# Reading a compressive memory with sixteen row-tiled products in place of four full ones, and keeping the memory on GpSimd

## The chip, the cores and the metric

The kernel runs on one core of one Trainium2 chip. The metric is the device time of one execution in microseconds (us); each comparison runs both kernels on the same chip.

## The reference, cut to what matters

A transformer layer: layer norm, attention with a compressive memory over four segments of 512 tokens (32 heads of 32 dimensions), then a gated MLP. Only the memory matters here.

```python
for s in range(4):                       # segments
    ...
    pq  = phi(qs)                        # phi(t) = t + 1 if t > 0 else exp(t)
    num = einsum('bhld,bhde->bhle', pq, M)
    den = einsum('bhld,bhd->bhl',  pq, z)[..., None] + 1e-06
    o   = g * (num / den) + (1 - g) * a_dot      # g: a gate per head
    M   = M + einsum('bhld,bhle->bhde', phi(ks), vs)
    z   = z + einsum('bhld->bhd', phi(ks))
```

## The kernel before

The heads are worked on in groups of four, which fill the 128 partitions: 8 groups a segment, 32 in all. I call them groups 0 to 31; groups 8 to 31 read the memory (24 reads), groups 0 to 23 add to it. A product in a *row tile* uses only 32 of the 128 rows (`tile_position` in the code says which); a *full-height* one uses all 128. The main loop interleaves group n's logits, group n-1's value read and state, and "filler" matmuls (projections of later groups, the output projection `wo`).

```python
def logits(n, rnd):                       # three rounds; each head is a 32-row tile with its own PSUM bank 0..3
    ...
            pe.matmul(PS[:, i, o:o + w], qk[32 * i:32 * (i + 1), 1, ...], qk[32 * i:32 * (i + 1), 0, ...],
                      start=True, stop=True, tile_position=(32 * i, 0))
    if rnd == 2 and n >= NQ:
        mem(n)
    act.activation(e[:, :, 0:wid], PS[:, 0:4, 0:wid], ACTF.Exp, scale=float(SCALE))
    ...  # causal mask on GpSimd (affine_select)
    if rnd == 2 and n >= NQ:
        mem_norm(n)

def mem(n):                               # block-diagonal memory: 128 rows x (4 heads x 33)
    c = n % NQ
    for cq in range(4):
        pe.matmul(PS[:, cq, 256:388], PQK[n % 2][:, 0, cq * 128:(cq + 1) * 128], MZB[:, c, :, 0:33],
                  start=True, stop=True)

def norm(n):                              # normalise the value read (PSUM banks 4 and 5), add the memory part
    ...  # VectorE: rd, rd, ta, otok

def state(n):
    ...
    b = next_bank()                       # banks 6 and 7 in turn, shared with the fillers
    for tcl in range(4):
        pe.matmul(PS[:, b, 0:132], PK[n % 3][:, tcl, :], V[:, tcl, 4 * c:4 * c + 4, 0:33], ...)
    if s == 0:
        dve.tensor_copy(MSUM[:, c, :], PS[:, b, 0:132])
    else:
        dve.tensor_tensor(MSUM[:, c, :], MSUM[:, c, :], PS[:, b, 0:132], ALU.add)
    dve.tensor_tensor(MZB[:, c, :, 0:33], MSUM..., MASKG[:, c, :, :], ALU.mult)

# main loop, group n:
    logits(n, 0); fill(f1); pv(n - 1)     # value read; ends with norm(n - 1)
    logits(n, 1); state(n - 1); fill(f2)
    logits(n, 2); fill(f3); fill(f4)      # f3 takes the bank that state() used
```

Waits are derived from a record of which 32-byte cells of on-chip memory (and which PSUM bank) each operation touched. And a PSUM bank counts as one thing: the filler behind the memory read may not start before VectorE has emptied the bank of the state product.

The softmax here doesn't subtract the row's maximum and nothing guards it: scores larger than these inputs give would overflow.

## Time and profile before

| | before |
|---|---|
| time, median | 801.87 us at first; 801.75 us with the runs beside the changed kernel |
| span in the profile | 800.1 us |
| first logit product to last (the attention stretch) | 283.45 us |
| 24 steps from last logit product over the memory read to the first filler | 11.43 us in all; 457 ns usually |

The head of the page of the kernel before, and its chain of waits:

```profile
span 800.1 us, 12483 instructions
...
PE 794.0 (99%) x5369; PEld 380.5 (48%) x5369; DVE 379.8 (47%) x769; ACT 297.6 (37%) x347; POOL 128.9 (16%) x241
...
PE 96%; DVE 3%; issue 0%; ACT 0%
```

TensorE (PE) sets the time; its queue is 96% of the path. A saving counts only if it shortens the queue of matmuls, and a delay elsewhere counts only if PE meets it.

The timeline of the kernel before at one memory read (start, duration, engine, operation, count):

```profile
152.71 0.29 PE L209 MATMUL ps<-qk 32*128 32x256 bf16 x4
...
152.93 0.41 PE L209 MATMUL ps<-mzb,pqk 128*128 128x132 bf16 x4
...
153.18 3.62 PE L209 MATMUL ps<-wv,xnT 128*128 128x512 bf16 x16
```

From the logits (152.71) to the filler (153.18) is 0.47 us; counted from the last of the four logit products, by single records, it is 457 ns: 210 to the first memory product, then 70, 59, 59 and 59.

The timeline of the kernel before at a read that came late (brackets: how long the engine was idle, and who ended it):

```profile
113.87 0.28 DVE L209 TENSOR_TENSOR msum<-msum,ps 128x132 f32<-128x132 f32 x1
114.19 0.30 DVE L209 TENSOR_TENSOR mzb<-msum,maskg 128x132 bf16<-128x132 f32 x1
114.20 1.36 POOL L209 TENSOR_SCALAR_AFFINE_SELECT e<-e 128x512 bf16<-128x512 bf16 x2 [2.51 <-ACT e L209]
...
114.21 0.29 PE L209 MATMUL ps<-qk 32*128 32x256 bf16 x4
...
114.54 0.23 PEld L209 LDWEIGHTS ps<-mzb,pqk 128*128 128x128 bf16 x4 [0.24 <-DVE mzb L209]
```

Group 11 reads the memory of its own heads, written eight groups earlier, yet it waits for the mask product of group 10, which ends at 114.49. The buffer has 272 bytes a group, not a multiple of 32, so a group and its neighbour share a cell. Four reads of 24 come 104 to 120 ns late this way.

The groups of instructions of the kernel before that the change touches (busy us, mean ns of one | idle us before):

```profile
L209 PE MATMUL ps<-mzb,pqk 128*128 128x132 bf16 x96 | 9.8, 225 | 0.2
...
L209 DVE TENSOR_TENSOR mzb<-msum,maskg 128x132 bf16<-128x132 f32 x24 | 7.5, 312 | 0.8
...
L209 DVE TENSOR_TENSOR msum<-msum,ps 128x132 f32<-128x132 f32 x16 | 4.5, 283 | 0.0
```

And the busy times of the kernel before in the stretch from the first logits of group 11 to those of group 13 (length, then busy us of each engine):

```profile
core 0: us, PE busy (x) PEld busy (x) DVE busy (x) ACT busy (x) POOL busy (x), PEclk, DMA share, GB/s
...
108.66:127.91 19.25, 19.20 (x194) 9.64 (x195) 17.68 (x41) 13.68 (x12) 7.44 (x14) 1.00 0.52 123
```

VectorE (DVE) is busy 17.68 us of 19.25 here, 92%, where its mean over the kernel is 47%.

### The profile page before, as it was taken

To read this page: it belongs to the slowest core of one execution; us is meant where nothing else is said; L and a number is where in the kernel's file an instruction comes from. 1 tells how busy PE (TensorE), PEld (TensorE's weight loads), DVE (VectorE), ACT (ScalarE), POOL (GpSimd) and SP (SyncE) were. 2 spreads that over 40 slices of the span, in tenths; PEclk is the share of its full clock that TensorE was granted. 3 is DMA by queue.
4 is the path that set the end of the run, shared out by engine and by line. 5 is a ranking of instruction groups with operands and counts; after the bars stand their busy time and mean duration, and the time that the engine had idled before them with its cause. 6 is when DMAs were issued, how large, how long until landed. Compare 5 with 4: busy or idle time off the path is not lost.

```text
span 800.1 us, 12483 instructions
## 1 busy us (share of the span) xinstructions
PE 794.0 (99%) x5369; PEld 380.5 (48%) x5369; DVE 379.8 (47%) x769; ACT 297.6 (37%) x347; POOL 128.9 (16%) x241
## 2 busy tenths in 40 slices
PE   8999999999999999999999999999999999999998
PEld 4454545555454445455544444444444444444444
DVE  6775688579844775844562000053234323323432
ACT  5777877787788675133333333100000000000000
POOL 3543333333333331100131000000000000000000
PEclk9999999999999999999999999999999999999999
DMA  9661535363515324511116000650270143021002
GB/s 294 180 161 53 93 81 122 84 106 86 92 31 127 113 54 114 157 47 53 53 53 132 1 0 1 205 105 7 79 132 1 33 116 69 0 66 47 1 7 86
DMA packets 125000, 64.79 MB, mean 81 GB/s; under 512 B 94992, under 2 KB 113936, under 8 KB 124944
## 3 DMA queue, kind: packets, MB, share of 16 engines
q1 hardware_dynamic: 124944, 63.99, 33.1%
q8 instruction: 42, 0.69, 0.4%
q14 instruction: 14, 0.11, 0.0%
HBM read 32.51 MB, written 8.39 MB: 51 GB/s over the span
## 4 chain that ended last, share of the span: by engine, by line
PE 96%; DVE 3%; issue 0%; ACT 0%
PE ps L209 96%; DVE stats L209 1%; DVE ta L209 0%; DVE otok L209 0%; DVE hch L209 0%; ACT e L209 0%; DVE rd L209 0%; DVE pqk L209 0%; DVE lno L209 0%; DVE mzb L209 0%; DVE etmp L209 0%; DVE mv L209 0%; DVE rdm L209 0%; DVE msum L209 0%; DVE xnT L209 0%
## 5 line engine op out<-in xcount | busy, mean ns | idle before, releaser
L209 PE MATMUL ps<-wspT,z 128*128 128x512 bf16 x896 | 194.0, 379 | 0.0
L209 ACT ACTIVATE e<-ps 128x2048 bf16<-128x2048 f32 (+1 forms) x96 | 152.8, 1591 | 49.5 <-PE ps L209 49.0
L209 PEld LDWEIGHTS ps<-wspT,z 128*128 128x128 bf16 x896 | 87.7, 98 | 105.7
L209 DVE TENSOR_TENSOR tmpg<-ps,brow 128x512 f32<-128x512 f32 x56 | 38.7, 691 | 197.1 <-DMA brow<-in_B_b_sp_dram 105.2
L209 POOL TENSOR_SCALAR_AFFINE_SELECT e<-e 128x512 bf16<-128x512 bf16 x128 | 83.5, 664 | 178.9 <-ACT e L209 178.7
L209 PE MATMUL ps<-win,hnT 128*128 128x448 bf16 x512 | 98.3, 352 | 0.0
L209 PE MATMUL ps<-w_out,yT 128*128 128x512 bf16 (+2 forms) x462 | 97.4, 373 | 0.0
L209 PE MATMUL ps<-hnT,win 128*128 128x512 bf16 x448 | 96.9, 379 | 0.0
L209 PEld LDWEIGHTS ps<-win,hnT 128*128 128x128 bf16 x512 | 49.8, 98 | 46.3 <-issue 0.2
L209 PEld LDWEIGHTS ps<-w_out,yT 128*128 128x128 bf16 x462 | 44.7, 98 | 52.4
L209 PEld LDWEIGHTS ps<-hnT,win 128*128 128x128 bf16 x448 | 43.9, 98 | 52.8
L209 PE MATMUL ps<-xnT,wk 128*128 128x512 bf16 x256 | 60.8, 380 | 0.0
L209 PE MATMUL ps<-xnT,wq 128*128 128x512 bf16 x256 | 60.6, 379 | 0.0
L209 PE MATMUL ps<-wv,xnT 128*128 128x512 bf16 x256 | 59.3, 379 | 0.1
L209 ACT ACTIVATE z<-ps 128x448 bf16<-128x448 f32 x60 | 32.5, 543 | 69.5 <-PE ps L209 69.5
L209 PE MATMUL ps<-wo,oT 128*128 128x512 bf16 x256 | 57.9, 379 | 0.0
L209 ACT ACTIVATE z1T<-ps 128x512 bf16<-128x512 f32 x56 | 33.4, 597 | 63.3 <-PE ps L209 63.3
L209 DVE TENSOR_TENSOR fin<-fin,ps 128x512 bf16<-128x512 bf16 (+2 forms) x33 | 22.2, 671 | 71.2 <-DMA fin<-out_dram 39.2
L209 DVE BATCH_NORM_STATS2 zst<-z 128x6 f32<-128x448 bf16 x64 | 38.9, 620 | 30.1 <-ACT z L209 30.1
L209 PEld LDWEIGHTS ps<-v,e 128*128 128x128 bf16 x1280 | 37.3, 96 | 9.1 <-issue 1.7
L209 DVE TENSOR_TENSOR yT<-tmpg,z1T 128x512 bf16<-128x512 f32 x56 | 38.8, 692 | 1.9
L209 PE MATMUL ps<-v,e 128*128 128x33 bf16 x1280 | 38.4, 177 | 0.0
(83 smaller groups left out, 576.1 us busy)
## 6 DMA issues: line engine op xcount, KB each, us to landing
xch<-in_A_x_dram SPq DMA_DIRECT2D x16, 256.0 KB, 3.0
xr<-in_A_x_dram SPq DMA_DIRECT2D x16, 256.0 KB, 3.5
out_dram<-hch SPq DMA_DIRECT2D x16, 256.0 KB, 2.5
fin<-out_dram SPq DMA_DIRECT2D x16, 256.0 KB, 2.7
out_dram<-fin SPq DMA_DIRECT2D x31, 128.0 KB, 1.7
win<-in_B_w_in_dram SPq DMA_DIRECT2D x4, 896.0 KB, 5.2
w_out<-in_B_w_out_dram SPq DMA_DIRECT2D x1, 3584.0 KB, 13.6
win<-in_B_w_in_dram SPq DMA_DIRECT2D x3, 1024.0 KB, 5.2
```

What stands on the lines that cost most here:

```text
L209: ins = getattr(e, op.name)(*op.args, **op.kw)
```

## The change

The intent: a head's memory block is 32x33, but the old product multiplies 128 rows by four heads' columns, three quarters of them zeros. Sixteen products of 32 rows by 33 columns, each in the row tile of its head, do only the real work, in the same tiling mode and banks as the logits before them. GpSimd takes over the running sum and condenses the block-diagonal memory to 33 columns.

```diff
-    MZB = cb("mzb", [128, NQ, 4, 34], BF16)
+    MZB = cb("mzb", [128, NQ, 48], BF16)
+    UPD, DGM, HALF2 = ...                                  # (shortened)
@@ mem
         for cq in range(4):
-            pe.matmul(PS[:, cq, 256:388], PQK[n % 2][:, 0, cq * 128:(cq + 1) * 128], MZB[:, c, :, 0:33],
-                      start=True, stop=True)
+            for i in range(4):
+                r = slice(32 * i, 32 * (i + 1))
+                pe.matmul(PS[:, i, 256 + 33 * cq:289 + 33 * cq], PQK[n % 2][r, 0, cq * 128:(cq + 1) * 128],
+                          MZB[r, c, 0:33], start=True, stop=True, tile_position=(32 * i, 0))
@@ mem_norm: the same three VectorE operations, with the q and i dimensions exchanged   # (shortened)
@@ state
-            dve.tensor_tensor(MSUM[:, c, :], MSUM[:, c, :], PS[:, b, 0:132], ALU.add)
-        dve.tensor_tensor(MZB[:, c, :, 0:33], MSUM..., MASKG[:, c, :, :], ALU.mult)
+            dve.tensor_copy(UPD[n % 2][:], PS[:, b, 0:132])
+            pool.tensor_tensor(MSUM[:, c, :], MSUM[:, c, :], UPD[n % 2][:], ALU.add)
+        pool.tensor_tensor(DGM[:], MSUM..., MASKG[:, c, :, :], ALU.mult)
+        pool.tensor_tensor(HALF2[:], DGM[:, 0:2, :], DGM[:, 2:4, :], ALU.add)
+        pool.tensor_tensor(MZB[:, c, 0:33], HALF2[:, 0, :], HALF2[:, 1, :], ALU.add)
```

More of the change, by code (lines that the diff above doesn't have):

```diff
@@ L311, in bass_sequential_preLN__memory_aug_infini_attn__mixer_gmlp__prompt_kernel @@
     MSUM = cb("msum", [128, NQ, 132], F32)
-    MZB = cb("mzb", [128, NQ, 4, 34], BF16)
+    MZB = cb("mzb", [128, NQ, 48], BF16)
+    UPD = [cb("upd%d" % i, [128, 132], F32) for i in range(2)]
+    DGM = cb("dgm", [128, 4, 33], F32)
+    HALF2 = cb("half2", [128, 2, 33], F32)
     MHALF = cb("mhalf", [128, 1], F32)
@@ L569, in mem @@
         for cq in range(4):
-            pe.matmul(PS[:, cq, 256:388], PQK[n % 2][:, 0, cq * 128:(cq + 1) * 128], MZB[:, c, :, 0:33],
-                      start=True, stop=True)
+            for i in range(4):
+                r = slice(32 * i, 32 * (i + 1))
+                pe.matmul(PS[:, i, 256 + 33 * cq:289 + 33 * cq], PQK[n % 2][r, 0, cq * 128:(cq + 1) * 128],
+                          MZB[r, c, 0:33], start=True, stop=True, tile_position=(32 * i, 0))
     def mem_norm(n):
-        om = PS[:, 0:4, 256:388].rearrange("p q (i d) -> p q i d", d=33)
+        om = PS[:, 0:4, 256:388].rearrange("p i (q d) -> p i q d", d=33)
+        tm = TM[n % 2][:].rearrange("p q i d -> p i q d")
         dve.tensor_single_scalar(RDM[:], om[:, :, :, 32], float(MEM_EPS), ALU.add)
         dve.reciprocal(RDM[:], RDM[:])
-        dve.tensor_tensor(TM[n % 2][:], om[:, :, :, 0:32], RDM[:].unsqueeze(3).to_broadcast([128, 4, 4, 32]), ALU.mult)
+        dve.tensor_tensor(tm, om[:, :, :, 0:32], RDM[:].unsqueeze(3).to_broadcast([128, 4, 4, 32]), ALU.mult)
     def norm(n):
@@ L604, in state @@
         else:
-            dve.tensor_tensor(MSUM[:, c, :], MSUM[:, c, :], PS[:, b, 0:132], ALU.add)
-        dve.tensor_tensor(MZB[:, c, :, 0:33], MSUM[:, c, :].rearrange("p (i d) -> p i d", d=33), MASKG[:, c, :, :],
-                          ALU.mult)
+            dve.tensor_copy(UPD[n % 2][:], PS[:, b, 0:132])
+            pool.tensor_tensor(MSUM[:, c, :], MSUM[:, c, :], UPD[n % 2][:], ALU.add)
+        pool.tensor_tensor(DGM[:], MSUM[:, c, :].rearrange("p (i d) -> p i d", d=33), MASKG[:, c, :, :], ALU.mult)
+        pool.tensor_tensor(HALF2[:], DGM[:, 0:2, :], DGM[:, 2:4, :], ALU.add)
+        pool.tensor_tensor(MZB[:, c, 0:33], HALF2[:, 0, :], HALF2[:, 1, :], ALU.add)
     def xr_load(tc):
```

## The prediction

> **What bounds it.** TensorE alone: the chain of waits is 96% matmuls, the busy table has PE at 99%, the granted clock is 1.00. In the attention part (20 to 320 us) I compared, in the order-of-time view, each start-to-start step between neighbouring groups of matmuls with the smallest of its kind: nearly nothing exceeds it, except four of the 24 memory reads, which start 104 to 120 ns late (0.46 us in all). VectorE (about 70% busy there), ScalarE (75%) and GpSimd (35%) have slack.
>
> **The memory read before.** From the last 256-column logit product to the first filler matmul takes 457 ns, 24 times: 210 ns to the first memory product (107 ns streaming, about 100 ns leaving the row-tiled mode; the Trainium skill, "TensorEngine Tiling (Array Packing)", Key Properties, says a mode switch drains the array, and switches in this trace cost 93 to 103 ns), then 70+59+59+59 ns for four 128x132 products.
>
> **After.** The products stay in the logits' mode; the switch comes after them: no drain is saved. Estimate: 109 ns to the first one (the 128-column logit round follows its 384-column one after 162 ns, stream time plus 2 ns). Row tiles start 3 to 4 ns apart in the logits, weight loads too, so four tiles take 8 x 3.5 = 28 ns (the 33-column value read: 25 ns each): three such steps plus 10 ns inside the last group, 95 ns; then 14 ns streaming and 93 ns drain. Sum 311 ns against 457: 146 ns x 24 = 3.5 us.
>
> **The four late reads.** At odd heads groups the old memory buffer (272 bytes a group) shares a 32-byte tracking cell with its neighbour, so the read waited for the neighbour's fresh write on VectorE. The new buffer has 96 bytes a group: this false wait goes, up to 0.46 us.
>
> **VectorE.** Loses the masking product (299 ns x 24, 7.5 us busy); the sum (283 ns) becomes a copy (285 ns). Off the path: worth nothing.
>
> **GpSimd.** Gains 88 small instructions, each waiting for the one before. Estimate from the 245 ns of a 128x1 operation in this trace plus 2.6 cycles per element for two inputs ("GPSIMD Engine Reference", Elementwise; no run shows it yet): 0.53, 0.53, 0.39, 0.32 us, with waits about 2 us a heads group, 1.4 in segment 0; some 40 us more busy. It sits before the last causal mask, whose slack to its use in the value read is 2.0 to 2.5 us in segment 0, 3.7 to 4.1 later; the mask slides 1.2 to 2 us. Off the path; segment 0 keeps about 1 us.
>
> **Prediction.** 801.9 - 3.5 - 0.4 = 798.0, plus a little for the unknown: 798.3 us, 80% range 797.5 to 801.0. Faster by over 2%: 0.5%; within 2%: 99%; slower by over 2%: 0.5%.
>
> **What would show it.** Step from last 256-column logit product to first filler about 310 ns in all 24; steps between groups of four near 28 ns; no late read; GpSimd near 170 us busy, VectorE near 372.
>
> **What would make it wrong.** Weight loads of row tiles sharing one path: groups then take about 55 ns and the gain halves (about 800 us). All sixteen spaced 25 ns: 15 x 25 + 216 = 591 ns, 3 us slower (about 805 us). GpSimd twice as slow as estimated: the last mask holds up the value read in segment 0, by tenths of a us, eight times.

## The result, and the profile after

| | before | after |
|---|---|---|
| time, median (range, 4 runs each) | 801.75 us (801.22 to 802.09) | 799.15 us (798.66 to 799.53) |
| span in the profile | 800.1 us | 797.3 us |
| attention stretch | 283.45 us | 280.91 us |
| 24 steps, sum | 11.43 us | 8.48 us |

The ratio is 0.9968, with a 95% interval of 0.9954 to 0.9982. The saving is real but small: 2.6 us by the medians, against the 3.6 us predicted (801.9 - 798.3).

The head of the page of the changed kernel, and its chain:

```profile
span 797.3 us, 13127 instructions
...
PE 790.4 (99%) x5657; PEld 378.9 (48%) x5657; DVE 377.3 (47%) x745; ACT 295.5 (37%) x347; POOL 170.6 (21%) x329
...
PE 96%; DVE 2%; ACT 1%; issue 0%; DMA 0%; DVEq 0%
```

The timeline of the changed kernel at one memory read:

```profile
161.43 0.29 PE L209 MATMUL ps<-qk 32*128 32x256 bf16 x4
...
161.55 0.26 PE L209 MATMUL ps<-mzb,pqk 32*128 32x33 bf16 x16
...
161.74 3.63 PE L209 MATMUL ps<-wv,xnT 128*128 128x512 bf16 x16
```

From logits to filler is now 0.31 us. By single records the step is 303 ns: 109 to the first memory product (no change of mode between them), 90 ns for all sixteen, 104 out to the filler. In a round of four different row tiles, starts are mostly 2 to 5 ns apart; the first round takes 28 to 29 ns, the next two 25 to 26. The first filler then needs 11 ns more than before to be followed by its second, so the full saving, measured to the second filler, is 529 ns against 673: 144 ns at each of 24 reads.

But four steps are longer. The timeline of the changed kernel at the worst of them, group 12:

```profile
123.01 0.69 DVE L209 TENSOR_TENSOR otok<-ta,tm 128x512 bf16<-128x512 f32 x1
...
123.24 0.26 PE L209 MATMUL ps<-mzb,pqk 32*128 32x33 bf16 x16
...
123.62 0.28 DVE L209 COPY upd<-ps 128x132 f32<-128x132 f32 x1
...
123.97 2.33 PE L209 MATMUL ps<-wo,oT 128*128 128x512 bf16 x10 [0.47 <-DVE upd L209]
```

The filler at 123.97 had to wait until VectorE copied the state product out of the bank (ends at 123.91; the copy stands behind `otok` in VectorE's queue). In the timeline of the kernel before, at the same group, the bank came free in time, though only just:

```profile
124.01 0.28 DVE L209 TENSOR_TENSOR msum<-msum,ps 128x132 f32<-128x132 f32 x1
...
124.11 0.41 PE L209 MATMUL ps<-mzb,pqk 128*128 128x132 bf16 x4
...
124.36 1.89 PE L209 MATMUL ps<-wo,oT 128*128 128x512 bf16 x8
```

VectorE left the bank at 124.29, 0.07 us before the filler began. A step shorter by 154 ns alone would have used that up.

The step is 838 ns in the changed kernel instead of 303, 835 at group 20, and 376 at groups 14 and 22: 1.22 us given back in all. That closes the account of the attention stretch, using the steps to the second filler: 24 x 144 ns and the 0.45 us of late reads are saved, 1.22 us is lost, 2.69 us net. The stretch holds 23 of the 24 steps; its 2.54 us is that sum less 0.14.

The new groups of the changed kernel (busy us, mean ns of one | idle us before):

```profile
L209 POOL TENSOR_TENSOR dgm<-msum,maskg 128x132 f32<-128x132 f32 x24 | 11.7, 488 | 1.3
...
L209 POOL TENSOR_TENSOR msum<-msum,upd 128x132 f32<-128x132 f32 x16 | 7.4, 461 | 0.0
L209 POOL TENSOR_TENSOR half<-dgm 128x66 f32<-128x66 f32 x24 | 7.2, 301 | 1.9
...
L209 PE MATMUL ps<-mzb,pqk 32*128 32x33 bf16 x384 | 6.3, 173 | 0.0
...
L209 POOL TENSOR_TENSOR mzb<-half 128x33 bf16<-128x33 f32 x24 | 5.8, 243 | 1.9
```

The matmul's busy time falls from 9.8 to 6.3 us, and GpSimd's four operations take 1.70 us a group from the first start to the last end (the three of segment 0, which has no sum, 1.2 to 1.3 us).

The busy times of the changed kernel from the first logits of group 11 to those of group 13:

```profile
core 0: us, PE busy (x) PEld busy (x) DVE busy (x) ACT busy (x) POOL busy (x), PEclk, DMA share, GB/s
108.14:127.52 19.38, 18.91 (x217) 9.53 (x216) 17.81 (x40) 13.49 (x12) 12.53 (x24) 1.00 0.59 124
```

VectorE lost a product of 0.3 us a group and is still busy 17.81 us of 19.38. One reason shows in the timeline of the changed kernel at group 11:

```profile
117.38 0.91 POOL L209 TENSOR_SCALAR_AFFINE_SELECT e<-e 128x512 bf16<-128x512 bf16 x1
...
117.83 1.00 DVE L209 TENSOR_TENSOR pqk<-pqk,etmp 128x1024 bf16<-128x1024 bf16 x1
```

The causal mask on GpSimd (0.63 us undisturbed) has slid behind the state operations and now lies over a VectorE maximum with two bf16 inputs; the maximum takes 1001 ns by its record (and 999 to 1001 at groups 13, 19 and 21). In the timeline of the kernel before, at this group, it took 693:

```profile
118.53 0.69 DVE L209 TENSOR_TENSOR pqk<-pqk,etmp 128x1024 bf16<-128x1024 bf16 x1
```

The Trainium skill's "GPSIMD Engine Reference", section 1 (Specifications), says that GpSimd's SBUF interfaces are shared with VectorE, with contention when a VectorE instruction has two SBUF inputs or uses both ports; this trace agrees, and puts 308 ns on this case. The traces also show who waits. VectorE's mask product ends 149 to 151 ns after a causal mask that was already running, whether this had begun 56 to 59 ns earlier (e2: the product takes 725 to 728 ns) or 439 to 694 ns earlier (before: 407 to 409 ns); where the causal mask began after it, the product kept its 298 to 299 ns. So in these cases the one that began second was held until the first was done, and how much that costs depends on the moment of the start.

### The profile page after: what moved, and what is told of

Same layout as the page of the kernel before. It is cut to its first block, busy times and chain, and to the rows that moved or that the text cites. A ratio compares the mean times of both kernels' runs of the same rounds, so it can differ in the third digit from the quotient of the medians.

```text
span 797.3 us, 13127 instructions
## 1 busy us (share of the span) xinstructions
PE 790.4 (99%) x5657; PEld 378.9 (48%) x5657; DVE 377.3 (47%) x745; ACT 295.5 (37%) x347; POOL 170.6 (21%) x329
## 4 chain that ended last, share of the span: by engine, by line
PE 96%; DVE 2%; ACT 1%; issue 0%; DMA 0%; DVEq 0%
PE ps L209 96%; DVE stats L209 1%; ACT e L209 0%; DVE lno L209 0%; DMA xch<-in_A_x_dram 0%; DVE hch L209 0%; DVE ta L209 0%; DVE otok L209 0%; ACT qk L209 0%; DVE rdm L209 0%; DVE mv L209 0%; DVE pqk L209 0%; DVE etmp L209 0%; DVE rd L209 0%; DVE upd L209 0%
## 5 line engine op out<-in xcount | busy, mean ns | idle before, releaser
L209 POOL TENSOR_SCALAR_AFFINE_SELECT e<-e 128x512 bf16<-128x512 bf16 x128 | 87.9, 699 | 129.5 <-ACT e L209 129.3
```

The lines of the kernel that those rows point to most:

```text
L209: ins = getattr(e, op.name)(*op.args, **op.kw)
```

## The experiments

"Late" below is the time by which a step of the PE queue exceeds the usual step of its kind, counted from 40 ns up. All runs gave correct results; all but the first two rows are of five rounds. "pk" is a wait for a DMA transpose in group 1, 0 to 1.2 us, that comes and goes between runs (so does the start-up, by 0.9 us); it is no part of the argument but is in the times.

| run | attention stretch | sum of 24 steps | late reads | late fillers | late elsewhere | median | ratio to before (95%) |
|---|---|---|---|---|---|---|---|
| before | 283.45 | 11.43 | 0.45 | 0 | 0 | 801.75 | |
| after | 280.91 | 8.48 | 0 | 1.22 | 0 | 799.15 | 0.9968 (0.9954, 0.9982) |
| e1_pe_old_buffer | 282.78 | 9.72 | 2.21 | 0.17 | pk 0.63 | 800.48 | 0.9991 (0.9979, 1.0004) |
| e2_pe_padded | 282.00 | 9.49 | 0 | 2.23 | pk 0.09 | 800.03 | 0.9979 (0.9965, 0.9992) |
| e3_pad_only | 283.02 | 10.98 | 0 | 0 | 0 | 801.10 | 0.9997 (0.9984, 1.0009) |
| e4_pool_only | 285.11 | 11.85 | 0 | 0.88 | pk 1.21 | 802.21 | 1.0010 (0.9997, 1.0022) |
| e5_tile_major | 281.66 | 9.05 | 0 | 0.93 | pk 0.21 | 799.46 | 0.9975 (0.9961, 0.9988) |
| e6_copy_first | 280.28 | 7.26 | 0 | 0 | pk 0.59 | 798.28 | 0.9957 (0.9944, 0.9969) |
| e7_pool_late | 281.08 | 8.33 | 0 | 1.04 | pk 0.31 | 798.54 | 0.9963 (0.9950, 0.9975) |
| e8_sum_first | 282.32 | 7.26 | 0 | 0 | 2.55, pk 0.07 | 799.87 | 0.9984 (0.9972, 0.9997) |
| e9_sum_first_pool_mask | 280.20 | 7.26 | 0 | 0 | pk 0.51 | 798.22 | 0.9959 (0.9946, 0.9971) |
| e10_pool_mask | 280.12 | 7.70 | 0 | 0.44 | 0 | 798.55 | 0.9963 (0.9950, 0.9977) |
| e11_order_only | 284.98 | 10.98 | 0 | 0 | 1.96 | 803.22 | 1.0020 (1.0008, 1.0033) |

My theory at the start: the gain is the shorter PE step alone, the loss is a late release of one PSUM bank by VectorE. Rivals: the relief of VectorE is the gain; or the removed false wait is.

### The parts alone

**e1_pe_old_buffer**: the kernel before with only the PE change. The block-diagonal buffer already holds each head's block in its own rows, so it needs no condensing:

```diff
+                pe.matmul(PS[:, i, 256 + 33 * cq:289 + 33 * cq], PQK[n % 2][r, 0, cq * 128:(cq + 1) * 128],
+                          MZB[r, c, i, 0:33], start=True, stop=True, tile_position=(32 * i, 0))
```

> The PE part alone: sixteen row-tiled products read the diagonal blocks straight out of the old block-diagonal buffer; VectorE sums and masks as before, GpSimd does nothing new. My theory (the gain is the shorter PE step alone): the step from last 256-column logit to first filler is about 303 ns where nothing is late. But the old buffer keeps the false wait on the neighbour's write, and the read now stands 100 ns earlier: about 100 ns at four odd groups, about 215 ns at the four late ones, 1.3 us in all; sum of the 24 steps 8.5 to 9.0 us (before 11.4, after 8.5), time about 799 us. Rival (the gain came from relieving VectorE of the mask and the sum): no gain here, about 801.7 us.

Measured: the undisturbed steps are 303 ns as expected, but the sum is 9.72 us, outside my range. The false wait costs 95 to 101 ns at four odd groups (as expected), 195 ns at groups 13 and 21 (about as expected), but 715 ns at groups 11 and 19. VectorE was much later there than I had assumed. By time alone this run does not differ from before (the interval holds 1).

**e2_pe_padded**: the same, and a buffer of 288 bytes a group:

```diff
-    MZB = cb("mzb", [128, NQ, 4, 34], BF16)
+    MZB = cb("mzb", [128, NQ, 4, 36], BF16)
```

> The same with the buffer padded to 288 bytes a group, so that no tracking cell is shared. My theory: all steps about 303 ns, except some 150 ns at the groups 12 and 20, where VectorE frees the bank late even before the change; sum of the 24 steps about 7.6 us, time about 797.9 us, that is about 1 us faster than the changed kernel, with no GpSimd work at all. Rival (GpSimd work is needed for the gain): not faster than 799 us.

Measured: no late read, 22 steps of about 303 ns, but 1416 and 1420 ns at groups 12 and 20, where I had expected 450. The run is 0.9 us slower than the changed kernel by the medians (of different rounds), not 1 us faster; its attention stretch is 1.09 us longer. So the expectation failed: of the 3.91 us that the short step (24 x 144 ns) and the end of the false wait (0.45) could bring, 2.23 us are lost without relief of VectorE. The timeline of this run shows where:

```profile
113.72 1.27 POOL L209 TENSOR_SCALAR_AFFINE_SELECT e<-e 128x512 bf16<-128x512 bf16 x2 [2.51 <-ACT e L209]
...
113.78 0.73 DVE L209 TENSOR_TENSOR mzb<-msum,maskg 128x132 bf16<-128x132 f32 x1
...
123.27 0.26 PE L209 MATMUL ps<-mzb,pqk 32*128 32x33 bf16 x16
...
124.24 0.28 DVE L209 TENSOR_TENSOR msum<-msum,ps 128x132 f32<-128x132 f32 x1
...
124.57 1.25 PE L209 MATMUL ps<-wo,oT 128*128 128x512 bf16 x5 [1.05 <-DVE msum L209]
```

Between these two places VectorE has no pause of note. The mask product takes 0.73 us, 0.4 more than its usual 0.30, because GpSimd's causal mask began 60 ns before it (in the kernel before it began 13 ns after it, and the mask product kept its 0.30). A layer-norm product at 120.09 also takes 0.82 us instead of 0.54. PE then waits for the sum at 124.24.

**e3_pad_only**: only the padding.

> The kernel before with nothing but the padding. My theory: the four late reads (104 to 120 ns each) go, all 24 steps 457 ns, sum 11.0 us instead of 11.4, time 0.46 us shorter, about 801.3 us: within noise of before. Rival (the false wait was most of the gain): about 799 us.

Measured: as expected in the trace. All 24 steps are 456 to 459 ns, the sum is 10.98 us, and the stretch is shorter by 0.43 us. The time cannot tell 0.4 us from nothing (0.9997, interval 0.9984 to 1.0009). The false wait was a small part of the gain.

**e4_pool_only**: long products as before, VectorE only copies, GpSimd sums and masks and does two dummy additions of the right sizes.

> The GpSimd part alone: four 128x132 products as before, padded buffer; VectorE only copies out of PSUM, GpSimd sums, masks, and makes two dummy additions of the sizes of the changed kernel. My theory: the GpSimd work gains nothing and costs late bank releases: about 380 ns at each of the groups 12 and 20 (536 minus the 154 ns by which the step is longer here), none at 14 and 22; sum of steps about 11.7 us, time about 802.0 us, GpSimd 170 us busy. Rival (relief of VectorE is the gain): 1 to 3 us faster than before.

Measured: late fillers of 439 ns at groups 12 and 20 (expected 380), nothing at 14 and 22, no gain. Without its 0.88 us of late fillers and the 1.21 us of pk, the stretch is 283.02 us, exactly that of the padding alone. So moving work off VectorE gains nothing by itself while PE's queue is long. (e3 says why: with the padding alone no step of the attention stretch is 40 ns late, so there was nothing for VectorE to give back.) The rival "relief of VectorE is the gain" falls. But e2 showed that the short products alone keep only part of theirs. The two parts of the change need each other, which neither my theory nor the rival had said.

### What the products cost

**e5_tile_major**: the two loops exchanged, four products of one row tile in a row.

```diff
-        for cq in range(4):
-            for i in range(4):
+        for i in range(4):
+            for cq in range(4):
```

> The changed kernel with the two loops of the sixteen products exchanged: four products of one row tile follow each other, then the next tile. Theory: tiles overlap only when neighbours in the queue are of different tiles; within one tile products follow at 25 ns as in the value read: 12 steps of about 25 ns and 3 of about 4 ns, so the step from logit to filler is about 109 + 310 + 107 = 525 ns instead of 303 (220 ns x 24 = 5.3 us), less about 1 us for the late bank releases that now hide: about 803.5 us. Rival (the order does not matter, the queue overlaps them all the same): steps stay at 303 ns, 799 us.

Measured: the usual step is 338 ns, 35 more than interleaved, not 220 more: sixteen starts in 124 ns, where the expectation had 310. So the expectation, built on the 25 ns between the full-height 33-column products of the value read, failed. Which half of it failed is open, because the records do not name the row tile and come sorted by start. They do show a pattern: in every one of the 24 reads, 13 of the 16 starts have another start 24 to 29 ns behind them; in the interleaved order, where each tile's next product is four places on, it is 12 of 16. That looks as if each tile still keeps some 25 ns between its own products, and the four tiles overlap in this order too, as the expectation's rival had it; it is not shown. Order matters a little (24 x 35 ns is 0.84 us), and the interleaved order of the change is the better one.

### Why the fillers are late

**e6_copy_first**: the changed kernel with VectorE's copy ahead of `norm` in its queue.

```diff
         if n > 0:
             state(n - 1)
+            norm(n - 1)          # no longer at the end of pv(n - 1), for groups of the first three segments
```

> The changed kernel with VectorE's copy of the state product (which frees the PSUM bank that the filler needs) ahead of the four normalising operations instead of behind them. Theory: the four late fillers (about 535 ns at groups 12 and 20, 75 ns at 14 and 22, 1.2 us in all) wait for that bank and nothing else; all 24 steps become 303 ns, sum 7.3 us instead of 8.5, time 1.2 us shorter than the changed kernel, about 797.9 us. Rival (they wait for some other work of VectorE or GpSimd that is just as late): the late steps stay.

Measured: all 24 steps are 301 to 303 ns, the sum 7.26 us. The late fillers are gone, and the stretch is 0.63 us shorter although 0.59 us of pk came in (1.22 us without it). The timeline of this run at group 12:

```profile
122.29 0.24 DVE L209 COPY upd<-ps 128x132 f32<-128x132 f32 x1
...
123.15 0.26 PE L209 MATMUL ps<-mzb,pqk 32*128 32x33 bf16 x16
...
123.35 2.98 PE L209 MATMUL ps<-wo,oT 128*128 128x512 bf16 x13
```

The copy now ends at 122.53, and the filler no longer waits. This shows that the fillers waited for that bank and nothing else.

**e7_pool_late**: the changed kernel with GpSimd's state operations behind the last causal mask.

```diff
         logits(n, 2)
+        if n > 0:
+            state_pool(n - 1)    # the four GpSimd operations; VectorE's copy stays where it was
```

> The changed kernel with GpSimd's four state operations behind the last causal mask instead of ahead of it. Theory A (the delayed mask runs into VectorE's bf16 operations, which stretches the 693 ns maximum at group 11 to 1000 ns, so VectorE is late at group 12): the mask no longer meets it, but the state operations, with two inputs each, may; if only the mask hurts, the 1000 ns operation is back at 693 and the late steps at 12 and 20 fall to about 150 ns. Theory B (VectorE waits for the layer-norm scale queued behind the state operations on GpSimd): the scale is still behind them, so the waits of VectorE for it stay near 8 us and the late steps stay near 535 ns.

Measured: the mask no longer meets the maximum, which is back at 693 ns. In the timeline of this run at group 11:

```profile
115.41 0.64 POOL L209 TENSOR_SCALAR_AFFINE_SELECT e<-e 128x512 bf16<-128x512 bf16 x1
...
117.78 0.69 DVE L209 TENSOR_TENSOR pqk<-pqk,etmp 128x1024 bf16<-128x1024 bf16 x1
```

The late fillers fall from 535 to 390 ns at groups 12 and 20, and 130 ns appear at groups 11 and 19: 1.04 us in all instead of 1.22. VectorE's waits for the layer-norm scale on GpSimd grew from 7.9 to 9.1 us in all, while lateness fell, so theory B, as a cause of the late fillers of the changed kernel, is not supported; there VectorE has no pause for the scale between the memory reads of groups 10 and 12. Theory A is supported in its mechanism but not in its size: I expected about 150 ns, and 390 stayed. The trace of e7 shows what holds VectorE instead: it idles 0.17 us for the scale before 109.63, and two minima, at 107.61 and 117.23, take 0.53 and 0.52 us where they take 0.42 in the changed kernel.

At this point I formed the theory that the later runs support: in groups 11 and 12, 19 and 20 VectorE's queue is nearly full, because the layer norms of two streams and the output projection's additions fall there. Once PE is faster by 144 ns a group, a stretched or added operation on VectorE there can reach PE, through whichever hand-over comes first (a hand-over is the point where PE needs a bank or an operand that VectorE has to finish with).

**e8_sum_first**: e2 with VectorE's sum ahead of `norm`, and its mask product behind it.

> The short products read from the padded block-diagonal buffer, no new GpSimd work; VectorE sums the state straight out of PSUM ahead of the normalising operations and masks it behind them. Theory (the filler waits for its PSUM bank, which VectorE frees late because its queue is nearly full in groups 11 and 12, 19 and 20: 18.8 us busy in 18.8 us there in the padded run): the bank is now free early, so all 24 steps are about 303 ns, sum 7.3 us instead of the 9.5 us of the padded run. A full VectorE may then show at another hand-over in those groups, 0 to 0.5 us each time. Time 797.8 to 798.5 us. Rival (without GpSimd's help the short product is not worth having): 800 us as in the padded run.

The "18.8 us in 18.8 us" of this expectation left out the 1.1 us in which PE stood still; with it the two groups of e2 last 19.96 us.

Measured: all 24 steps are 301 to 304 ns, yet the attention stretch is 2.04 us longer than in e6. The lateness moved: 627 ns before the first logits of groups 12 and 20, about 220 and 270 ns before the next filler of the neighbouring groups (0.22 + 0.63 + 0.27 us, twice), and 110 ns at three groups of segment 0. The waits of this run:

```profile
PEld ps L209 <- DVE tm L209: 4.2, 7, 1.1
...
PE ps L209 <- DVE tm L209: 1.1, 2, 0.6
```

Here the first logits of a group wait for `tm`, the memory's normalisation of the group before, which still reads their banks. I had allowed 0 to 0.5 us each time; it is 1.1 us. The expected sum of steps was right, the expected time was not (799.87 against 797.8 to 798.5).

**e11_order_only**: the same order and padding with the long products of the kernel before.

> The kernel before with the padded buffer and the sum ahead of the normalising operations, long products kept. Theory: with the long product the bank was already free in time, so the order alone is worth nothing: all 24 steps 457 ns, sum 11.0 us, time about 801.2 us, as with the padding alone. Rival (the order brings the gain of the earlier-copy run by itself): 799 us or less.

Measured: all 24 steps are 457 ns as expected, but 1.96 us is late elsewhere, and the run is slower than the kernel before (803.22, ratio 1.0020, interval 1.0008 to 1.0033). My expectation that the order is worth nothing was wrong: it does harm. VectorE now waits for the state product before it may normalise, where before it did the normalising first; in the full groups that time is missing later. (The waits show the first part; that the second follows from it is my reading.)

**e9_sum_first_pool_mask**: e8 with the mask product on GpSimd, one operation instead of four.

```diff
-        dve.tensor_tensor(MZB[:, c, :, 0:33], MSUM..., MASKG[:, c, :, :], ALU.mult)     # behind norm()
+        pool.tensor_tensor(MZB[:, c, :, 0:33], MSUM..., MASKG[:, c, :, :], ALU.mult)
```

> The same with the one masking product given to GpSimd (about 0.46 us a group there, 0.3 us less on VectorE). Theory: all 24 steps 303 ns, and no late hand-over elsewhere, since VectorE keeps 0.3 us a group free: sum 7.3 us, time about 797.7 us, the fastest. If the help of GpSimd costs more than it brings (its last mask is 0.5 us later and meets VectorE's bf16 operations), it is slower than the one before.

Measured: all steps 302 to 304 ns, nothing late but 0.51 us of pk. The same order that lost 2.55 us in e8 loses nothing once VectorE has this one product less. Median 798.22 us.

**e10_pool_mask**: e2 with the mask product on GpSimd and the old order.

> The padded run with the masking product on GpSimd, and the old order on VectorE. Theory (a full VectorE makes the late fillers): VectorE has 0.3 us a group less to do, so the late steps at 12 and 20 fall from 1416 ns to 600 to 1100 ns, sum of steps 7.9 to 8.9 us; time about 799 us. Rival (VectorE's load does not matter, only where the copy stands in its queue): they stay at 1416 ns.

Measured: 522 and 526 ns at groups 12 and 20 instead of 1416 and 1420, sum 7.70 us, a little better than my range. The timeline of this run at group 12:

```profile
122.80 0.26 PE L209 MATMUL ps<-mzb,pqk 32*128 32x33 bf16 x16
122.87 0.28 DVE L209 TENSOR_TENSOR msum<-msum,ps 128x132 f32<-128x132 f32 x1
...
123.21 1.69 PE L209 MATMUL ps<-wo,oT 128*128 128x512 bf16 x7 [0.15 <-DVE msum L209]
```

So VectorE's load counts, beside the place of the release in its queue (e6 changed only that). This run also sizes the collision in the changed kernel. Here one GpSimd operation stands before the mask instead of four, the maximum of group 11 takes 691 ns, and the filler is 220 ns late; in the changed kernel it is 535 ns late and the maximum took 310 ns longer. The difference of 315 ns is that stretch: counted from group 10's memory read, VectorE's operations of the two runs start within 0.01 us of each other up to this maximum, and 0.31 to 0.32 us apart from there to the release of the bank.

Three variants have shorter attention stretches than the changed kernel (e6, e9, e10: 280.1 to 280.3 us against 280.91), and better medians (798.2 to 798.6). Their intervals overlap that of the changed kernel, and they were not run in the same rounds with it, so by time alone "faster than the change" is not shown. By trace, e6 and e9 leave no late step of VectorE's making.

## Why the prediction was right or wrong

**Right: what bounds the kernel, and the step.** The change is worth what it does to PE's queue. I predicted 311 ns for the usual step and 146 ns a read; the trace shows 303 ns, and 144 ns when the slower start of the filler is counted. The round of four tiles was estimated at 28 ns and took 28 to 29 the first time, then 25 to 26. The drain stayed, as said. (The Trainium skill, "TensorEngine Tiling (Array Packing)", Key Properties, says that switching the mode drains the array; this trace agrees: the step from the last 33-column tiled product to the full-height filler is 104 ns, of which some 14 ns are its streaming, at the 216 ns of a 512-column product.)

**Right: the false wait.** All four late reads went; e3 puts 0.43 us on it (0.4 predicted).

**Right: GpSimd's totals.** 170.6 us busy (predicted near 170), the mask's slack in segment 0 is 1.3 to 1.4 us (predicted about 1), and PE never waited for GpSimd directly.

**Wrong: "VectorE ... Off the path: worth nothing."** This is the step that failed; it is why 2.6 us came and not 3.6. In groups 11 and 12 VectorE was already 92% busy (groups 19 and 20 repeat them), and I had averaged over 75 us. With PE faster, VectorE's release of the state product's bank became the later of the two, 1.22 us in all at four fillers (e6 shows that it is this bank). The relief that I called worthless was needed: without it (e2) 2.23 us is lost, with it alone (e4) nothing is won, with one product less on VectorE (e10) 0.44 us is lost. The prediction had named three things that would make it wrong; none of them happened, and this one was not among them. Its 0.3 us "for the unknown" rested on no trace, so that 2.6 us is not farther from 3.6 owes something to luck.

**Wrong: GpSimd as "off the path".** Not through its own results but through its place in time: its four operations pushed the mask onto VectorE's maximum, 308 ns of VectorE's time at group 11. I had only asked whether GpSimd would be late for its own consumers.

**Mis-sized:** the two-input operations on GpSimd were estimated at 0.53, 0.53, 0.39 and 0.32 us; they took 0.46, 0.49, 0.30 and 0.24. My estimate added the 0.245 us of a one-column operation to the 2.6 cycles per element of the Trainium skill's "GPSIMD Engine Reference", section 3.1 (Elementwise). As I used it, that slope was 2.2 ns an element (0.285 us for 132). From 66 to 132 elements the mean of the mask and sum grows by about 0.17 us, 2.6 ns an element, and from 33 to 66 by 58 ns, 1.8 ns; so the slope is about right, and the fixed part that I added is what was too large.

What stays open: how the time splits between stretched and merely late operations at each group of VectorE was not measured apart, except for the 308 ns above.

## What to carry to other kernels

When the bottleneck gets faster by a little at one place, look for the engine that is fullest in the same few microseconds, not on average: window the busy times by the loop's own iterations. A bank or buffer is freed by the last operation of somebody's in-order queue; where that operation stands in the queue, and how full the queue is, decide together; in e8, moving it without making room only moved the wait. And before building a condensed copy of an operand, look whether the products can read it where it lies: the block-diagonal memory already had each head's block in the rows of its tile.

## What the Trainium skill lacked or had wrong

- "TensorE: Matmul & The Clock Gate", section "Wait — 56ns, not 53.3ns?": it states that start-to-start never drops below about 25 ns however small the product. For full-height products this agrees (33 columns: 25 ns). It does not say that this leaves out row tiles: products of different row tiles start 2 to 5 ns apart here, sixteen in 90 ns interleaved and in 124 ns tile by tile (e5). Interleaved, a round of four takes 25 to 29 ns, so within each tile the floor may still hold (not shown).
- "TensorEngine Tiling (Array Packing)", Key Properties: it names the drain at a mode switch but no size. Here, beyond the streaming time, it is about 90 to 103 ns. The first full-width product straight behind row-tiled ones, long or short, is followed 11 ns later than usual (226 to 227 ns instead of 215 to 216); so are the two late fillers of e4, which stand behind full-height products.
- "GPSIMD Engine Reference", section 1: it names the contention with VectorE without a size; other passages of the skill say more about it, so this only adds numbers. Here a VectorE maximum of two bf16 inputs went from 693 to 1001 ns, a two-input f32 product of 132 columns from 0.30 to 0.73 us, and GpSimd's own mask from 0.63 to 0.91 us.
